# A planner that orders the work behind an attention stage, with new intervals, and a last token tile in two column halves

## The chip, the core and the metric

The kernel runs on one core of one Trainium2 chip. The metric is the device time of one execution, in microseconds. The core's engines, by the names that the profile uses: PE (TensorE, the matmuls; PEld is its weight load), DVE (VectorE), ACT (ScalarE), POOL (GpSimd), and SP, which issues the DMAs here (SPq is its queue). Each engine works through a list of instructions in the order that the program fixed for it, and waits where an instruction's inputs or its buffer are not there yet.

## The reference

A banded attention with a bias over 2 x 8 heads (576 positions, head size 64) gives 1152 tokens of 512 numbers. They pass a mixture of four experts, and then a gated network behind an RMS norm:

```python
def _moe_ref(x, domain_probs, w1, w2):          # x 1152x512, w1 4x512x1024, w2 4x1024x512
    p = domain_probs / (domain_probs.sum(-1, keepdims=True) + 1e-09)
    for e in range(E):
        h = np.maximum(x @ w1[e], 0.0)
        out += p[:, e:e + 1] * (h @ w2[e])

def _moe2_ref(x, w_gate, w_val, w_out, rms_g):  # d_ff 1536
    rms = np.sqrt(np.mean(x * x, axis=-1, keepdims=True) + 1e-06)
    xn = x / rms * rms_g
    g = xn @ w_gate
    silu = g * (1.0 / (1.0 + np.exp(-g)))
    return (silu * (xn @ w_val) @ w_out).astype(np.float32)
```

## The kernel before, in words

**Attention** fills the first 74 us. Its order is written out by hand (class Flow); nothing here touches it.

**Behind it** stand 1152 tokens as 9 tiles of 128. The four experts are done in two halves of the hidden width each, which gives eight units u = 0 to 7. A unit has hidden products (512 hidden columns from all tokens) and out products (`out_plain`: for each token tile 12 matmuls of 128x512 into one bank of PSUM, L1168, which `mix` then adds into y with a weight, L1198). The hidden products of u = 1 to 7 go as Strassen products: `products` (L1032 on) makes four blocks of a 2x2 product from seven block products of six matmuls of 128x288 each (L1050), in four banks `ps_a` to `ps_d`, with sums by DVE between them: `x` and `r` are SBUF tiles that take banks and earlier sums, and the next matmuls of a block wait for its bank to be read (`r<-ps_c,x` is a DVE addition, L798, that reads bank c). Then comes the norm (`finish`, `transposes`, with ACT's Sqrt and Square), and the gated network: its first part, `plain_unit_0`, is plain (`gated`: 12 matmuls of 128x384 from `gemm_in`, L285, for gate and value, Silu on ACT, L1355, a product on DVE, L1359), the rest is Strassen again, and three out products (u = 0 to 2) follow, of which the second and third are added into `acc` by DVE (L798) and the third stored tile by tile (`out_y`, L1420).

**Splits.** Every matmul operand is split in a high part in a short float form, which ACT copies (L802, `wa<-raw`, `wb<-raw`, `xh<-ps_b`), and a low part, which DVE gets by subtraction (L795, `wa<-raw,wa`, `xl<-ps_b,xh`). The weights come by DMA into two buffers `raw`, of 512 KB a load, from `in_w` (the experts') or from `f` (the gated network's). Those of the gated network are 64-bit floats first; ACT and three DVE instructions turn each piece of them (`scratch`) into 32-bit ones in a tile `stage` (L977, then L980, L983 and L986 one on the other's result), and a DMA stores it to `f`.

**What sets the order.** Class `Plan` (L53 to 148) keeps a time for each of PE, DVE, ACT and SP while the program is written. Work that PE's next matmuls wait for is placed at once (`now`, `pe`); splits, weight conversions, norm steps and loads are put down with a due time (`later`) and fill places where the planner expects an engine free (`step`, `drain`). An instruction is taken to occupy its engine for `START` + n x `RATE`, and its result to be there `LAT` after that for whatever needs it:

```python
    LAT = 0.1
    START = {"d": 0.16, "a": 0.19, "q": 0.2}
    RATE = {"d": 1 / 960, "a": 1 / 1200, "q": 0.0025}
```

The planner has no entry for the reload of ACT's function table, which the compiler puts in where the functions of two ACT instructions need different tables (ACT_TABLE_LOAD). What comes out is a fixed list for each engine; no time of the planner is in the kernel itself.

Of the kernel before, what the change touches and what calls it, by code (L numbers as in the profile page):

```python
# [21 lines left out]
NT, DM = B * S, H * D  # L22
# [19 lines left out]
class End:  # L42


    def __init__(self, t=math.inf):
        self.own, self.of = t, None

    @property
    def t(self):
        return self.own if self.of is None else max((x.t for x in self.of), default=0.0)  # L50


class Plan:  # L53

    LAT = 0.1
    START = {"d": 0.16, "a": 0.19, "q": 0.2}
    RATE = {"d": 1 / 960, "a": 1 / 1200, "q": 0.0025}

    def __init__(self, free):
        self.t = 0.0
        self.free = {e: max(0.0, free[e] - free["t"]) for e in "daq"}
        self.jobs = []

    def cost(self, e, n):
        return self.START[e] + n * self.RATE[e]

    def ready(self, needs):
        return max((x.t + self.LAT for x in needs), default=0.0)  # L70

    def best(self, job):
        ready = self.ready(job[2])
        if job[6]:
            ready = max(ready, min(x.t for x in job[6][0]) + self.LAT)
        if ready == math.inf:
            return None
        ends = []
        for e in job[0]:
            start = max(self.free[e], ready)  # L80
            ends.append((start + self.cost(e, job[1]), start, e))
        return min(ends)[1:]

    def step(self, until, only=None, due=None):

# [21 lines left out]
        return True  # L107

    def issue(self, e, n, needs, emit, end):
        start = max(self.free[e], self.ready(needs))  # L110
        emit(e)
        self.free[e] = start + self.cost(e, n)
        end.own = self.free[e] + (2.0 if e == "q" else 0.0)

    def later(self, engines, n, needs, emit, due, buffer=None):

# [2 lines left out]
        return end  # L119

    def settle(self, needs):
        while self.ready(needs) == math.inf:
            assert self.step(math.inf)

    def drain(self, until):
# [1 line left out]
            pass  # L127

    def now(self, e, n, needs, emit, slack=None):
        self.settle(needs)  # L130
        ready = self.ready(needs)
        self.drain(min(ready, max(self.t, self.free[e])))
        while self.step(ready, e):
            pass
        if slack is not None:
            while self.step(max(ready, self.free[e]) + 0.01, e, self.t + slack):
                pass
        end = End()
        self.issue(e, n, needs, emit, end)
        return end  # L140

    def pe(self, n, cols, needs, emit):
        self.settle(needs)
        start = max(self.t, self.ready(needs))
# [80 lines left out]
def tile_fused(ctx: ExitStack, tc: tile.TileContext, qS, kS, vS, probs, w1, w2, wgv, wo, g, out):  # L225
# [585 lines left out]
    class Issued:  # L811


        def __init__(self, end):
            self.end = end

        @property
        def t(self):
            return self.end.t - 2.0 - pl.LAT

    loads = {"raw": [], "t": []}

# [197 lines left out]
    def any_bank(half=0, leave=False):  # L1020

        turn["ps"] += 1
        if leave:
            return bank(min(("bd", "ac")[(turn["pr"] + 1) % 2], key=lambda tag: min(x.t for x in rings[tag])))
        if held or turn["busy"]:
            return bank(("ba", "dc")[half][turn["pr"] % 2])
        tags = ["abcd"[(turn["ps"] + i) % 4] for i in range(4)]
        return bank(min(tags, key=lambda tag: min(x.t for x in rings[tag])))
# [127 lines left out]
            reading[g].append(end)  # L1156
        return w, end, da

    def out_plain(parts, w, t, put, last=()):

        a, end, da = parts
        ps, need, done = any_bank(leave=t > NTT - 3)

        def emit():
            n = 0
            for k in range(4):
                for s, i in ((0, 0), (0, 1), (1, 0)):
                    nc.tensor.matmul(ps, lhsT=a(s)[:, k, :], rhs=w[k][0]()[:, i, :], start=(n == 0), stop=(n == 11))  # L1168
                    n += 1

        k = pl.pe(12, DM, [end, need] + [x[1] for x in w], emit)
        done.of = [put(t, slice(0, DM), ps, [k])]
        da.of = [k]
        for e in last:
            e.of = [k]

    def out_tiles(w, put, parts, ahead, between=lambda t: None, last=()):

        for t in range(NTT):
            for i in range(t, min(t + ahead + 1, NTT)):  # L1180
                if i not in parts:
                    parts[i] = plain_parts(i, pl.t + 2.7 * (i - t))
            out_plain(parts.pop(t), w, t, put, last if t == NTT - 1 else ())
            between(t)
# [110 lines left out]
    for u in range(1, NU):  # L1295
# [173 lines left out]
```

## Time and profile before

| | |
|---|---|
| time, median of 3 runs | 653.48 us (653.34 to 653.51) |
| time of the profiled execution | 653.97 us |
| its span in the profile | 652.2 us |
| PE busy | 644.9 us (99%) |
| DVE busy | 505.8 us (78%) |
| ACT busy | 317.1 us (49%) |
| POOL busy | 43.6 us (7%) |
| granted TensorE clock | 1.00 in every stretch |
| chain that ended last | PE 98%, DMA 1% |

The times in the rows are microseconds from the start of the span. The span is 1.8 us shorter than the profiled execution's own time; the rest lies around the program.

### The profile page before, as it was taken

The numbers are of one execution on the slowest core, as the hardware profiler recorded it, in microseconds if no ns is written. First come the engines' busy times: TensorE is split into PE (matmuls) and PEld (weight loads), VectorE is DVE, ScalarE is ACT, GpSimd is POOL, SyncE is SP. The second block draws the span as 40 slices with busy tenths as digits, with TensorE's granted clock in tenths as the row PEclk, the third lists the DMA queues.
The fourth block names the chain that finished last, engine by engine and source line by source line (L and its number), as shares of the span: only waits on it lengthen the run. The fifth ranks groups of instructions, "written<-read, shape, count | busy, mean of one in ns | idle before, by whom it ended". The sixth has DMA issues, their size and how long they took to land.

```text
span 652.2 us, 11044 instructions
## 1 busy us (share of the span) xinstructions
PE 644.9 (99%) x4166; PEld 583.0 (89%) x4166; DVE 505.8 (78%) x1113; ACT 317.1 (49%) x726; POOL 43.6 (7%) x94
## 2 busy tenths in 40 slices
PE   7999999999999999999999999999999999999997
PEld 5688899989989989889889889889998999899986
DVE  7987677788888898897888887888776388847672
ACT  7988364633635535535435535874445335213330
POOL 6865000000000000000000000000000000000000
PEclk9999999999999999999999999999999999999999
DMA  8542014154433624625525334011111101000012
GB/s 266 172 135 64 1 66 129 33 159 144 165 131 119 207 96 146 193 81 173 167 91 181 101 118 145 32 63 64 66 34 64 65 1 66 33 1 33 33 50 96
DMA packets 24229, 64.95 MB, mean 100 GB/s; under 512 B 2672, under 2 KB 5488, under 8 KB 24176
## 3 DMA queue, kind: packets, MB, share of 16 engines
q1 hardware_dynamic: 23888, 63.96, 29.8%
q8 instruction: 32, 0.52, 0.3%
q10 hardware_dynamic: 288, 0.30, 0.1%
q14 instruction: 21, 0.17, 0.1%
HBM read 52.45 MB, written 11.80 MB: 99 GB/s over the span
## 4 chain that ended last, share of the span: by engine, by line
PE 98%; DMA 1%; DVE 0%; issue 0%; SPq 0%
PE ps_a L1168 14%; PE ps_c L1050 11%; PE ps_d L1050 11%; PE ps_d L1168 9%; PE ps_b L1168 8%; PE ps_c L1168 8%; PE ps_b L1050 8%; PE ps_a L1050 8%; PE ps_b L285 3%; PE a L653 2%; PE ps_c L285 2%; PE pst L550 2%; PE ps_d L285 2%; PE po L569 2%; PE ps_a L285 2%; PE a L684 2%
## 5 line engine op out<-in xcount | busy, mean ns | idle before, releaser
L1168 PE MATMUL ps_a<-wa,op 128*128 128x512 f32 x408 | 96.5, 390 | 0.0
L1168 PEld LDWEIGHTS ps_a<-wa,op 128*128 128x128 f32 x408 | 76.4, 188 | 15.8
L802 ACT ACTIVATE op<-h 128x512 fp32r<-128x512 f32 x95 | 57.6, 626 | 59.0 <-PE ps_d L1168 24.7
L802 ACT ACTIVATE wb<-raw 128x512 fp32r<-128x512 f32 (+1 forms) x98 | 49.9, 536 | 39.8 <-DVE raw L795 39.6
L795 DVE TENSOR_TENSOR op<-h,op 128x512 fp32r<-128x512 f32 x95 | 63.7, 685 | 2.7 <-ACT op L802 2.4
L1168 PE MATMUL ps_d<-wa,op 128*128 128x512 f32 x252 | 59.1, 389 | 0.0
L1168 PE MATMUL ps_b<-wa,op 128*128 128x512 f32 x240 | 56.6, 391 | 0.0
L795 DVE TENSOR_TENSOR wb<-raw,wb 128x512 fp32r<-128x512 f32 (+1 forms) x98 | 54.6, 575 | 2.4 <-ACT wb L802 2.1
L1168 PE MATMUL ps_c<-wa,op 128*128 128x512 f32 x240 | 56.3, 390 | 0.0
L1168 PEld LDWEIGHTS ps_d<-wa,op 128*128 128x128 f32 x252 | 47.2, 188 | 9.8
L1168 PEld LDWEIGHTS ps_c<-wa,op 128*128 128x128 f32 x240 | 45.0, 188 | 9.3
L1168 PEld LDWEIGHTS ps_b<-wa,op 128*128 128x128 f32 x240 | 44.6, 188 | 9.1
L795 DVE TENSOR_TENSOR wa<-raw,wa 128x512 fp32r<-128x512 f32 (+1 forms) x50 | 31.8, 651 | 13.2 <-ACT wa L802 13.2
L1050 PE MATMUL ps_c<-xh,wb 128*128 128x288 f32 x160 | 38.6, 297 | 0.0
L1050 PE MATMUL ps_d<-xh,wb 128*128 128x288 f32 x160 | 38.6, 296 | 0.0
L1050 PE MATMUL ps_a<-xh,wb 128*128 128x288 f32 x160 | 38.3, 294 | 0.0
L1050 PE MATMUL ps_b<-xh,wb 128*128 128x288 f32 x160 | 38.2, 294 | 0.0
L802 ACT ACTIVATE wa<-raw 128x512 fp32r<-128x512 f32 (+1 forms) x50 | 27.8, 597 | 18.6 <-DMA raw<-in_w 16.0
L1111 ACT ACTIVATE h<-r 128x576 f32<-128x576 f32 x28 | 19.2, 686 | 30.8 <-DVE r L798 30.8
L798 DVE TENSOR_TENSOR r<-ps_c,x 128x288 f32<-128x288 f32 x44 | 20.1, 457 | 17.5 <-PE ps_c L1050 15.2
L795 DVE TENSOR_TENSOR raw<-raw 128x256 f32<-128x256 f32 x66 | 27.7, 419 | 0.7
L1050 PEld LDWEIGHTS ps_b<-xh,wb 128*128 128x128 f32 x160 | 27.8, 188 | 0.4
(264 smaller groups left out, 1523.2 us busy)
## 6 DMA issues: line engine op xcount, KB each, us to landing
raw<-in_w SPq DMA_DIRECT2D x32, 512.0 KB, 3.8
scratch<-in_wgv SPq DMA_DIRECT2D x24, 512.0 KB, 4.5
f<-stage SPq DMA_DIRECT2D x36, 256.0 KB, 2.5
raw<-f SPq DMA_DIRECT2D x18, 512.0 KB, 3.2
scratch<-in_wo SPq DMA_DIRECT2D x12, 512.0 KB, 4.5
out_y<-acc SPq DMA_DIRECT2D x9, 256.0 KB, 2.0
vt<-in_vS SPq DMA_DIRECT2D x4, 512.0 KB, 5.4
qt<-in_qS SPq DMA_DIRECT2D x7, 288.0 KB, 4.1
```

The costliest lines, as they stand in the source:

```text
L285: nc.tensor.matmul(ps, lhsT=a, rhs=x[:, k, tok], start=(n == 0), stop=(n == 3 * KC - 1))
L550: nc.tensor.transpose(pst[:w, j, :], tts[n % 2][:, 2 * kb + j, c0 : c0 + w], ident)
L569: nc.tensor.matmul(po[r, kb * P : kb * P + len(range(blocks.shape[1])) * P], lhsT=vt[:, kb, v], rhs=blocks[:, :, 1:3, :] if j else blocks[ ...
L653: nc.tensor.matmul(box[0], lhsT=a, rhs=x[:, k, tok], start=k == 0 and a is wh and x is xh, stop=k == 3 and a is wl)
L684: nc.tensor.matmul(box[0], lhsT=tile[0][:, x, k, :], rhs=v[:, i, :], start=k == 0 and x == i == 0, stop=k == 3 and x == 1)
L795: EN[e].tensor_tensor(out=out, in0=a, in1=b, op=ALU.subtract)
L798: EN[e].tensor_tensor(out=out, in0=a, in1=b, op=ALU.add)
L802: nc.scalar.activation(out=out, in_=a, func=AF.Copy)
L1050: nc.tensor.matmul(ps, lhsT=s[:, k, :], rhs=t(k), start=start and m == 0, stop=m == 5, skip_group_check=True,)
L1111: return wrote(gr, pl.now("a", tok.stop - tok.start, needs + was_reading[gr], lambda e: nc.scalar.activation(out=h[:, c, tok], in_=src, fu ...
L1168: nc.tensor.matmul(ps, lhsT=a(s)[:, k, :], rhs=w[k][0]()[:, i, :], start=(n == 0), stop=(n == 11))
```

## The change

The planner gets other numbers. `LAT` goes from 0.1 to 0.04. `START` becomes `HOLD`, the interval after which the engine takes its next instruction: 0.07 in place of 0.16 for DVE, 0.09 in place of 0.19 for ACT. `MORE` is how much later than that the result is there for another engine: 0.085 for DVE, 0.1 for ACT, 2.0 for a DMA, 0.17 for PE (0 before). A new method `seen` asks which engine needs a result: on the engine that made it, it is taken to be there as soon as that engine takes its next instruction.

```diff
-    LAT = 0.1
-    START = {"d": 0.16, "a": 0.19, "q": 0.2}
+    LAT = 0.04
+    HOLD = {"d": 0.07, "a": 0.09, "q": 0.2}
+    MORE = {"d": 0.085, "a": 0.1, "q": 2.0, "t": 0.17}
     RATE = {"d": 1 / 960, "a": 1 / 1200, "q": 0.0025}
...
+    def seen(self, e):
+
+        if self.of is not None:
+            return max((x.seen(e) for x in self.of), default=0.0)
+        return self.hold if e == self.e and e is not None else self.own + Plan.LAT
...
     def cost(self, e, n):
-        return self.START[e] + n * self.RATE[e]
-
-    def ready(self, needs):
-        return max((x.t + self.LAT for x in needs), default=0.0)
+        return self.HOLD[e] + (n[e] if isinstance(n, dict) else n) * self.RATE[e]
+
+    def ready(self, needs, e):
+        return max((x.seen(e) for x in needs), default=0.0)
...
-        end.own = self.free[e] + (2.0 if e == "q" else 0.0)
+        end.own, end.e, end.hold = self.free[e] + self.MORE[e], e, self.free[e]
...
         self.t = start + n * (cols / 2400 + 0.013)
-        return End(self.t)
+        return End(self.t + self.MORE["t"], "t", self.t)
```

The out products get a width. The last token tile of the last unit (u = 2, tile 8) is done as two halves of 256 columns: 24 matmuls of 128x256 in place of 12 of 128x512, two DVE additions of 128x256, two stores of 128 KB. `out_first` is new too, and nothing calls it.

```diff
-    def out_plain(parts, w, t, put, last=()):
+    def out_plain(parts, w, t, put, last=(), width=DM, leave=False, begun=None):
 
         a, end, da = parts
-        ps, need, done = any_bank(leave=t > NTT - 3)
+        for c0 in range(0, DM, width):
...
+            k = pl.pe(12, width, [end, need] + [x[1] for x in w], emit)
+            done.of = [put(t, c, ps[:, :width], [k])]
...
-        out_tiles(right_o, put, parts, 3, last=o_read)
+        out_tiles(right_o, put, parts, 3, last=o_read, width=DM // 2 if u == NV - 1 else DM)
```

PE's list keeps its order, but for that last tile, and POOL's is the same. The lists of DVE, ACT and SP are ordered anew behind the attention. Line numbers move: L795, L798, L802 of before are L804, L807, L811 of the change; L980, L983, L986 are L992, L995, L998; L1267, L1272, L1355, L1359 are L1303, L1308, L1391, L1395. Three places follow.

**Place A: DVE in the first block product of u = 1**, at about 102 to 109 us. The rows with `ps_b` and `ps_d` are the sums that PE's next block product waits for; the others split weights. Before:

```order
L798 TENSOR_TENSOR x<-ps_b,x 128x288
L798 TENSOR_TENSOR r<-ps_d,x 128x288
L798 TENSOR_TENSOR r<-ps_d,r 128x288
L795 TENSOR_TENSOR wb<-raw,wb 128x512
L795 TENSOR_TENSOR wa<-raw,wa 128x512
L798 TENSOR_TENSOR r<-ps_d,x 128x288
```

With the change:

```order
L804 TENSOR_TENSOR wb<-raw,wb 128x512 x2
L804 TENSOR_TENSOR wa<-raw,wa 128x512 x2
L807 TENSOR_TENSOR x<-ps_b,x 128x288
L804 TENSOR_TENSOR wa<-raw,wa 128x512
L807 TENSOR_TENSOR r<-ps_d,x 128x288
L807 TENSOR_TENSOR r<-ps_d,r 128x288
L804 TENSOR_TENSOR wa<-raw,wa 128x512
```

Two subtractions of `wb` and two of `wa` now stand directly ahead of the sums, and one `wa<-raw,wa` stands between `x<-ps_b,x` and `r<-ps_d,x`.

**Place B: DVE in a hidden product of u = 2**, at about 159 to 171 us; two like it follow in u = 3 and u = 4. L980, L983 and L986 (L992, L995, L998) are the three steps on a `stage`, `op<-h,op` splits the left side of an out product. Before, from `r<-ps_c,r` on (the list then goes on with `x<-ps_d,x`, L983, L980, `x<-ps_a,x`, `r<-ps_c,x`, `r<-ps_c,r`, L986):

```order
L798 TENSOR_TENSOR r<-ps_c,r 128x288
L986 SCALAR_TENSOR_TENSOR stage<-scratch,stage 128x512
L983 SCALAR_TENSOR_TENSOR stage<-scratch,stage 128x512
L798 TENSOR_TENSOR r<-ps_c,x 128x288
L798 TENSOR_TENSOR x<-ps_c,x 128x288
L986 SCALAR_TENSOR_TENSOR stage<-scratch,stage 128x512
L798 TENSOR_TENSOR x<-ps_b,x 128x288
L798 TENSOR_TENSOR r<-ps_d,x 128x288
L798 TENSOR_TENSOR r<-ps_d,r 128x288
L795 TENSOR_TENSOR op<-h,op 128x512 x2
L980 TENSOR_SCALAR stage<-stage 128x512
L798 TENSOR_TENSOR r<-ps_d,x 128x288
```

With the change, the same stretch:

```order
L807 TENSOR_TENSOR r<-ps_c,r 128x288
L995 SCALAR_TENSOR_TENSOR stage<-scratch,stage 128x512
L998 SCALAR_TENSOR_TENSOR stage<-scratch,stage 128x512
L992 TENSOR_SCALAR stage<-stage 128x512
L995 SCALAR_TENSOR_TENSOR stage<-scratch,stage 128x512
L807 TENSOR_TENSOR r<-ps_c,x 128x288
L807 TENSOR_TENSOR x<-ps_c,x 128x288
L998 SCALAR_TENSOR_TENSOR stage<-scratch,stage 128x512
L807 TENSOR_TENSOR x<-ps_b,x 128x288
L807 TENSOR_TENSOR r<-ps_d,x 128x288
L804 TENSOR_TENSOR op<-h,op 128x512
L807 TENSOR_TENSOR r<-ps_d,r 128x288
```

and directly behind it:

```order
L804 TENSOR_TENSOR op<-h,op 128x512
L992 TENSOR_SCALAR stage<-stage 128x512
L995 SCALAR_TENSOR_TENSOR stage<-scratch,stage 128x512
L998 SCALAR_TENSOR_TENSOR stage<-scratch,stage 128x512
L807 TENSOR_TENSOR r<-ps_d,x 128x288
L807 TENSOR_TENSOR x<-ps_d,x 128x288
L992 TENSOR_SCALAR stage<-stage 128x512
L995 SCALAR_TENSOR_TENSOR stage<-scratch,stage 128x512
L807 TENSOR_TENSOR x<-ps_a,x 128x288
L807 TENSOR_TENSOR r<-ps_c,x 128x288
L998 SCALAR_TENSOR_TENSOR stage<-scratch,stage 128x512
L807 TENSOR_TENSOR r<-ps_c,r 128x288
```

Between the first `r<-ps_c,r` and the last `r<-ps_c,x` shown there are now ten steps on a `stage` where there were six, with the same nine sums and the same two splits of `op`; and one step, L998, stands ahead of the last `r<-ps_c,r`, where it (L986) stood behind.

**Place C: ACT and DVE in the plain part of the gated network**, at about 436 to 446 us. `xh` and `xl` are the two parts of the normalized tokens, which PE's next gate and value products read; `y<-y,rstd` scales a token tile; `sg` is Silu, `h` the product behind it. ACT before:

```order
L802 ACTIVATE xh<-ps_c 128x4x128 x2
L1267 ACTIVATE v<-v 128x3
L1355 ACT_TABLE_LOAD
L1355 ACTIVATE sg<-ps_d 128x384
L1272 ACTIVATE y<-y,rstd 128x512 x2
L802 ACTIVATE xh<-ps_b 128x4x128
L802 ACTIVATE xh<-ps_a 128x4x128
L802 ACTIVATE xh<-ps_d 128x4x128
L1355 ACTIVATE sg<-ps_a 128x384
```

ACT with the change:

```order
L1303 ACTIVATE v<-v 128x3
L811 ACTIVATE xh<-ps_c 128x4x128 x2
L1308 ACTIVATE y<-y,rstd 128x512
L1391 ACT_TABLE_LOAD
L1391 ACTIVATE sg<-ps_d 128x384
L1308 ACTIVATE y<-y,rstd 128x512
L811 ACTIVATE wa<-raw 128x512 x2
L811 ACTIVATE xh<-ps_b 128x4x128
L811 ACTIVATE xh<-ps_a 128x4x128
L811 ACTIVATE xh<-ps_d 128x4x128
```

The second scaling and two copies of `wa<-raw` now stand between the Silu `sg<-ps_d` and the three copies of `xh`. DVE before:

```order
L1359 TENSOR_TENSOR h<-ps_b,sg 128x384
L795 TENSOR_TENSOR wb<-raw,wb 128x512 x2
L795 TENSOR_TENSOR xl<-ps_b,xh 128x4x128
L795 TENSOR_TENSOR xl<-ps_a,xh 128x4x128
L795 TENSOR_TENSOR xl<-ps_d,xh 128x4x128
L795 TENSOR_TENSOR scratch<-xh 128x576
```

DVE with the change:

```order
L1395 TENSOR_TENSOR h<-ps_b,sg 128x384
L804 TENSOR_TENSOR wa<-raw,wa 128x512 x2
L804 TENSOR_TENSOR scratch<-xh 128x576
L807 TENSOR_TENSOR scratch<-scratch,xl 128x576
L804 TENSOR_TENSOR xl<-ps_b,xh 128x4x128
L804 TENSOR_TENSOR xl<-ps_a,xh 128x4x128
L804 TENSOR_TENSOR xl<-ps_d,xh 128x4x128
```

Two subtractions of `wa` and two sums into `scratch` stand ahead of the three subtractions of `xl`, where two subtractions of `wb` stood.

## Rows read from the trace of the kernel before

**Rows 1.** Busy time by stretch: us, each engine's busy time (x instructions), PE clock, DMA

```profile
73.90:648.50 574.60, 574.60 (x3425) 528.28 (x3423) 445.86 (x854) 259.55 (x523) 0.00 (x0) 1.00 0.29 95
```

**Rows 2.** The chain that ended last, at the end: start, us, what

```profile
645.81 2.73 PE ps_a L1168 x12
...
648.56 0.69 DVE acc L798
```

**Rows 3.** The page's groups and DMA issues (median us to landing)

```profile
L798 DVE TENSOR_TENSOR r<-ps_c,x 128x288 f32<-128x288 f32 x44 | 20.1, 457 | 17.5 <-PE ps_c L1050 15.2
...
raw<-f SPq DMA_DIRECT2D x18, 512.0 KB, 3.2
...
out_y<-acc SPq DMA_DIRECT2D x9, 256.0 KB, 2.0
```

**Rows 4.** DVE in order of time, 158 to 170 us: start, us, what

```profile
159.56 0.46 DVE L798 TENSOR_TENSOR r<-ps_c,r 128x288 f32<-128x288 f32 x1 [0.32 <-PE ps_c L1050]
159.93 0.68 DVE L986 SCALAR_TENSOR_TENSOR stage<-scratch,stage 128x512 int32<-128x512 int32 x1
...
161.95 0.46 DVE L798 TENSOR_TENSOR r<-ps_c,x 128x288 f32<-128x288 f32 x1 [0.74 <-PE ps_c L1050]
162.44 0.46 DVE L798 TENSOR_TENSOR x<-ps_c,x 128x288 f32<-128x288 f32 x1
...
163.79 0.46 DVE L798 TENSOR_TENSOR x<-ps_b,x 128x288 f32<-128x288 f32 x1 [0.29 <-ACT x L802]
164.36 0.46 DVE L798 TENSOR_TENSOR r<-ps_d,x 128x288 f32<-128x288 f32 x1
...
168.99 0.42 DVE L980 TENSOR_SCALAR stage<-stage 128x512 int32<-128x512 int32 x1
```

**Rows 5.** PE in order of time, two matmuls at 171 to 172 us

```profile
171.30 0.29 PE L1050 MATMUL ps_c<-xh,wb 128*128 128x288 f32 x1
...
172.10 0.96 PE L1050 MATMUL ps_c<-t,wb 128*128 128x288 f32 x6
```

**Rows 6.** ACT in order of time, 436 to 445 us

```profile
436.19 1.09 ACT L802 ACTIVATE xh<-ps_c 128x512 fp32r<-128x512 f32 x2 [1.34 <-PE ps_c L1288]
...
437.39 1.28 ACT L1355 ACT_TABLE_LOAD   x1
438.68 0.50 ACT L1355 ACTIVATE sg<-ps_d 128x384 f32<-128x384 f32 x1
439.07 1.33 ACT L1272 ACTIVATE y<-y,rstd 128x512 f32<-128x512 f32 x2
441.23 0.60 ACT L802 ACTIVATE xh<-ps_b 128x512 fp32r<-128x512 f32 x1 [0.83 <-PE ps_b L1288]
...
444.23 1.15 ACT L802 ACTIVATE wa<-raw 128x512 fp32r<-128x512 f32 x2 [1.04 <-DMA raw<-f]
```

**Rows 7.** DVE in order of time, 439 to 446 us

```profile
439.69 1.28 DVE L795 TENSOR_TENSOR wb<-raw,wb 128x512 fp32r<-128x512 f32 x2
...
443.07 0.68 DVE L795 TENSOR_TENSOR xl<-ps_d,xh 128x512 fp32r<-128x512 f32 x1
...
444.80 0.75 DVE L798 TENSOR_TENSOR scratch<-scratch,xl 128x576 f32<-128x576 f32 x1
445.58 0.76 DVE L795 TENSOR_TENSOR scratch<-scratch,xl 128x576 f32<-128x576 f32 x1
```

**Rows 8.** PE in order of time, one matmul at 444 us

```profile
444.19 0.33 PE L285 MATMUL ps_c<-xl,wb 128*128 128x384 f32 x1
```

**Rows 9.** ACT at 101 us and PE at 108 us, in order of time

```profile
101.33 0.69 ACT L1196 ACTIVATE y<-ps_c,pn_sb 128x512 f32<-128x512 f32 x1 [0.36 <-PE ps_c L1168]
...
107.76 0.29 PE L1050 MATMUL ps_d<-xh,wb 128*128 128x288 f32 x1
```

**Rows 10.** DMA issues in 107 to 109 us, then in 155 to 159 us

```profile
raw<-in_w SPq DMA_DIRECT2D x2, 512.0 KB, 5.5
...
raw<-in_w SPq DMA_DIRECT2D x1, 512.0 KB, 3.6
```

More of the change, by code (lines that the diff above doesn't have):

```diff
@@ L42, with __init__ @@
 class End:
-    def __init__(self, t=math.inf):
+    def __init__(self, t=math.inf, e=None, hold=None):
         self.own, self.of = t, None
+        self.e, self.hold = e, hold
     @property
@@ L63, in __init__ @@
         self.free = {e: max(0.0, free[e] - free["t"]) for e in "daq"}
-        self.jobs = []
+        self.jobs, self.slack = [], None
     def cost(self, e, n):
-        return self.START[e] + n * self.RATE[e]
-    def ready(self, needs):
-        return max((x.t + self.LAT for x in needs), default=0.0)
+        return self.HOLD[e] + (n[e] if isinstance(n, dict) else n) * self.RATE[e]
+    def ready(self, needs, e):
+        return max((x.seen(e) for x in needs), default=0.0)
     def best(self, job):
[L73 to L77, printed above, removed]
         ends = []
         for e in job[0]:
+            ready = self.ready(job[2], e)
+            if job[6]:
+                ready = max(ready, min(x.seen(e) for x in job[6][0]))
             start = max(self.free[e], ready)
             ends.append((start + self.cost(e, job[1]), start, e))
-        return min(ends)[1:]
+        end = min(ends)
+        return None if end[0] == math.inf else end[1:]
     def step(self, until, only=None, due=None):
@@ L109, in issue @@
     def issue(self, e, n, needs, emit, end):
-        start = max(self.free[e], self.ready(needs))
+        start = max(self.free[e], self.ready(needs, e))
         emit(e)
         self.free[e] = start + self.cost(e, n)
-        end.own = self.free[e] + (2.0 if e == "q" else 0.0)
+        end.own, end.e, end.hold = self.free[e] + self.MORE[e], e, self.free[e]
     def later(self, engines, n, needs, emit, due, buffer=None):
@@ L121, in settle @@
     def settle(self, needs):
-        while self.ready(needs) == math.inf:
+        while self.ready(needs, None) == math.inf:
             assert self.step(math.inf)
@@ L129, in now @@
     def now(self, e, n, needs, emit, slack=None):
+        slack = self.slack if slack is None else slack
+        slack = self.slack if slack is None else slack
         self.settle(needs)
-        ready = self.ready(needs)
+        ready = self.ready(needs, e)
         self.drain(min(ready, max(self.t, self.free[e])))
@@ L143, in pe @@
         self.settle(needs)
-        start = max(self.t, self.ready(needs))
+        start = max(self.t, self.ready(needs, "t"))
         self.drain(start)
@@ L818, in t, with seen @@
         def t(self):
-            return self.end.t - 2.0 - pl.LAT
+            return self.end.t - Plan.MORE["q"] - pl.LAT
+        def seen(self, e):
+            return self.end.t - Plan.MORE["q"]
     loads = {"raw": [], "t": []}
@@ L1157, in plain_parts, with emit, out_tiles, out_first @@
         return w, end, da
-    def out_plain(parts, w, t, put, last=()):
+    def out_plain(parts, w, t, put, last=(), width=DM, leave=False, begun=None):
         a, end, da = parts
-        ps, need, done = any_bank(leave=t > NTT - 3)
+        for c0 in range(0, DM, width):
+            ps, done = begun or (None, None)
+            need = End(0.0)
+            if not begun:
+                ps, need, done = any_bank(leave=leave)
+            c = slice(c0, c0 + width)
+            def emit():
+                n = 0
+                for k in range(4):
+                    for s, i in ((0, 0), (0, 1), (1, 0)):
+                        nc.tensor.matmul(ps[:, :width], lhsT=a(s)[:, k, :], rhs=w[k][0]()[:, i, c], start=not (n or begun), stop=(n == 11))
+                        n += 1
+            k = pl.pe(12, width, [end, need] + [x[1] for x in w], emit)
+            done.of = [put(t, c, ps[:, :width], [k])]
+        da.of = [k]
+        for e in last:
+            e.of = [k]
+    def out_tiles(w, put, parts, ahead, between=lambda t: None, last=(), width=DM, tiles=(0, NTT), begun={}):
+        for t in range(*tiles):
+            for i in range(t, min(t + ahead + 1, tiles[1])):
+                if i not in parts:
+                    parts[i] = plain_parts(i, pl.t + 2.7 * (i - t))
+            end = t == NTT - 1
+            out_plain(parts.pop(t), w, t, put, last if end else (), width if end else DM, t > tiles[1] - 3, begun.get(t))
+            between(t)
+    def out_first(parts, w, tag, last):
+        a, end, da = parts
+        ps, need, done = bank(tag)
         def emit():
@@ L1167, in emit @@
                 for s, i in ((0, 0), (0, 1), (1, 0)):
-                    nc.tensor.matmul(ps, lhsT=a(s)[:, k, :], rhs=w[k][0]()[:, i, :], start=(n == 0), stop=(n == 11))
+                    nc.tensor.matmul(ps, lhsT=a(s)[:, k, :], rhs=w[k][0]()[:, i, :], start=(n == 0), stop=False)
                     n += 1
         k = pl.pe(12, DM, [end, need] + [x[1] for x in w], emit)
-        done.of = [put(t, slice(0, DM), ps, [k])]
         da.of = [k]
@@ L1175, in out_plain @@
             e.of = [k]
[L1177 to L1184, printed above, removed]
+        return ps, done
     mixed = {}
@@ L1231, in tile_fused @@
             parts[t + 2] = plain_parts(t + 2, pl.t + 2)
-        out_plain(parts.pop(t), v, t, lambda *a: mix(0, *a), [w2_read] if t == NTT - 1 else [])
+        out_plain(parts.pop(t), v, t, lambda *a: mix(0, *a), [w2_read] if t == NTT - 1 else [], leave=t > NTT - 3)
     ss = const.tile([P, NTT], F32, name="ss")
```

## The prediction

> **What bounds the kernel now.** I read the busy time by stretch first. Behind the attention, from 73.9 to 648.5 us, PE is busy for 574.60 of 574.60 us at a granted clock of 1.00 [rows 1]. So in this stretch there is no idle time of PE that a better order of the other engines could take away, and none that could swallow a new wait: as PE's list keeps its order and its shapes up to the last token tile, each 0.1 us by which a sum, a split or a load comes late at PE is 0.1 us at the end. DVE with 528.28 us comes close, but it is not the bound. Next I read the end of the chain of waits: the last 12 matmuls take 2.73 us from 645.81, the last addition on DVE 0.69 us from 648.56, and the store (median 2.0 us from issue to landing) fills nearly all that is left up to 652.2 [rows 2, 3]. Only here can time be won. For the new order I then took the three places where the lists of the change put other work ahead of something that PE needs soon, and walked along them with the durations of before.
>
> **The tail, part by part.** Twelve matmuls of 512 columns take 2.73 us, 0.2275 each [rows 2]; six of 288 take 172.10 - 171.30 = 0.80, 0.133 each [rows 5]. On the line through both, one of 256 takes 0.133 - 32 x 0.00042 = 0.120, and 24 take 2.88: PE ends 0.15 later. The addition that remains behind it has 256 columns in place of 512. Between 457 ns at 288 and 690 at 512 [rows 2, 3] the slope is 1.04 ns a column, so it takes 0.42: 0.27 earlier. The first half's addition and store have 1.4 us of matmuls to lie behind. The last store moves 128 KB in place of 256. At worst its 2.0 us stay, at best it shrinks as from 512 KB (3.2) to 256 KB (2.0) [rows 3], by half of 1.2, 0.6. The number of its rows stays 128 and only their length is halved, so I stand nearer to the first: 0.2. The sum is 0.15 - 0.27 - 0.2 = **-0.3 us** (-0.1 to -0.7).
> The Trainium skill, "Perfetto Trace Analysis", section DMA Optimizations, speaks against this: small DMAs (under 2 KB) have significant overhead for each transfer. The halved rows are 1 KB long. By it the store would keep its 2.0 us and the tail would win 0.1; no row of before shows a store of such rows.
>
> **Place C, 436 to 446 us, once.** Before, ACT made `xh<-ps_c` twice and the root from 436.19 to 437.39, then the table reload (1.28), then Silu at 438.68; `xh<-ps_b` waited 0.83 us for PE and started at 441.23 [rows 6]; the subtractions followed, the last one `xl<-ps_d` from 443.07 for 0.68, to 443.75 [rows 7]; PE took its result at 444.19 [rows 8]. That is 0.44 of slack. With the change ACT's list reads: root and two `xh` (to 437.39), `y<-y,rstd` (0.61: two take 1.33 and the second of a pair runs out in some 0.7), reload 438.00 to 439.28, Silu (0.39 to the next, from 438.68 to 439.07), second `y` at 439.67, `wa<-raw` at 440.28 and, 0.52 on (a pair takes 1.15, one 0.63), at 440.80, and the three `xh` only then, from 441.32, 0.50 apart [rows 6]. The load for these `wa` isn't late: its buffer comes free 6 us sooner, as two subtractions of `wb` that followed Silu (439.69) [rows 7] now stand ahead of the norm. DVE's list has two `wa` first: the first copy ends at 440.91, so 440.93 and 0.60 on 441.53 (a pair takes 1.28, one 0.68), then a sum into `scratch` at 442.13, and one that needs its result 0.78 on, at 442.91 (444.80 to 445.58 in the rows), then 0.68 with the change of operands `xl<-ps_b` 443.59, `xl<-ps_a` 444.19, `xl<-ps_d` 444.79, done 445.47 [rows 7]. PE starts some 0.05 later, at 445.52 against 444.19: **1.3 us**. If the two sums went at 0.60 and 0.60 it would be 1.0; if the second scaling takes 0.70 and the sums 0.78, 1.5. What makes it late is that the reload, 1.28 us, isn't in the planner's numbers, and that the margins which covered it (0.16 and 0.19 an instruction) are halved.
> The Trainium skill, "ScalarE: Activation LUTs", section What ACT_TABLE_LOAD costs, gives 1283 ns for a reload and another 1380 ns for a drain with each switch. The reload agrees with the row to the digit (1.28), the drain doesn't: Silu follows the reload within 0.01 us here [rows 6]. By the rule with its drain place C would cost 2.7 (estimate from that page).
>
> **Place B, 159 to 171 us, in u = 2, 3 and 4.** I start at `r<-ps_c,r`, 159.56, which waits for PE in both lists. Intervals: a sum 0.37 to the next instruction (159.56 to 159.93), 0.49 to a sum that needs it (161.95 to 162.44), 0.57 from an `x` to the `r` that needs it (163.79 to 164.36), a step of 512 or a split 0.60, with its dependent step behind it 0.72 (0.68 and a wait), L980 0.45 to the step that needs it (0.42 and a wait) [rows 4, 7]. The list of the change gives: 159.93 L995, 160.65 L998, 161.25 L992, 161.70 L995, 162.30 `r<-ps_c,x` (161.95 before), 162.79 `x<-ps_c,x`, then as before 1.35 to `x<-ps_b,x`, 164.14, `r<-ps_d,x` 164.71, split 165.08, `r<-ps_d,r` 165.68, split 166.05, L992 166.65, L995 167.10, L998 167.82, `r<-ps_d,x` 168.42, `x` 168.91, L992 169.28, L995 169.73, `x<-ps_a,x` 170.33, `r<-ps_c,x` 170.90, done 171.36. PE then starts at 171.41; before it did so at 171.30 [rows 5]. L998 follows at 171.27, and with it ahead of it `r<-ps_c,r` goes from 171.87 to 172.33; PE at 172.38, where 172.10 + 0.11 was due [rows 5]: 0.17 more. That is 0.28 a unit, 0.84 for three; in u = 5 to 7 one split stands where L992 and L995 precede `x<-ps_a,x`, and no step between the two `r<-ps_c`, so the walk is 0.45 shorter there and I take nothing but 0.03 each: **0.9 us**. Of four added steps (some 2.4 us) 1.5 goes into waits of DVE for PE (0.32 and 0.74 among them [rows 4]). If dependent steps go at 0.60 nothing is left; if each step takes 0.02 more, 0.4 a unit: 0 to 1.2.
>
> **Place A, 102 to 109 us, once.** A `wa<-raw,wa` stands ahead of `r<-ps_d,x`, and its `raw` must land first. The load is issued when the two `wb` subtractions have freed the buffer. Their copies stand ahead of ACT's `y<-ps_c`, 101.33 [rows 9], so they end at about 102.3. A load of 512 KB alone takes 3.6 us, one of a pair 5.5 [rows 10] (3.2 is the median from `f` [rows 3]); SP's list has a load shortly ahead of this one and another shortly behind, so I take 4.4, between the two: landed 106.7. Behind it come the copy 0.65, the subtraction 0.62, the sum 0.46 and PE's 0.05: 108.5 against 107.76 [rows 9], **0.8 us** (0 at 3.6, 1.9 at 5.5). All else that waits on DVE there waits too, the next sums among it, but PE needs them later.
>
> **The sum.** 0.8 + 0.9 + 1.3 - 0.3 = +2.7 us. Against the profiled execution's own 653.97 us that is 656.7, of a span of 654.9; that execution lies 0.5 above the median of the three runs, 653.48, so I predict **656.2 us**. The bounds add up to +0.3 (A and B nothing, C 1.0, tail -0.7) and +4.5.
>
> **The rivals.**
> *The planner's intervals hold (not slower).* If a dependent instruction on the same engine starts after the shorter interval and a load lands in 3.5 us, A and B leave nothing. C keeps about 1.2 of its reload: +0.9, 654.4 us, within what a measurement of this kernel can tell from no change (0.2%, 1.3 us). It decides from a sum of stalls below 1.6. For it: at B only 0.1 to 0.2 is missing, and at A all hangs on one load. Against it: 0.78 from one `scratch` sum to the next, which the shorter interval would make 0.67 [rows 7]. If ACT found a gap for the reload as well, 653.2.
> *Loads land late.* At 5.5 A costs 1.9, so 657.3; with another late load elsewhere 658 and more. For it: the pair of rows 10 and ACT's wait of 1.04 for `raw<-f` [rows 6]. Against it: the queue of before is mostly free.
> *The reload costs twice.* ACT could be emptied around a reload at a place where, other than before, a scaling stands directly ahead of it: once more its 1.28 us [rows 6], place C 2.6, 657.5. Silu's start at 438.68, right behind the reload, speaks against it. This is what the Trainium skill's page "ScalarE: Activation LUTs" says of the drain, above.
> *Faster.* The tail alone, with the best store, gives 652.8, which isn't 1.3; for more PE would have to run closer than in rows 1, at full busy time.
>
> **How the numbers follow.** The forecast with stalls at two or three places has 0.62, the planner's intervals 0.17, late loads 0.14, the reload twice 0.04, a gain beyond the tail 0.03. The first has 655.0 to 657.0 as its own range. To leave out no more than 2 in 10 the range goes from 654.6 (near the rival without A and B) to 657.9 (A at its upper end, 657.3, and 0.6 for a second late load): the unknown costs make it 3.3 wide. Slower by over 0.2% are the forecast, late loads and the reload, 0.80; within it the planner's intervals, 0.17; faster 0.03.
>
> **What would show it.** In the trace of the changed kernel PE should have idle time before `ps_c<-xl` at C of 1.0 to 1.5, released by DVE's `xl<-ps_d`; before a matmul into `ps_d` at A of 0 to 1.9, released by `r<-ps_d,x` with ACT's `wa<-raw` waiting for `raw<-in_w` ahead of it; and three pairs of 0.1 and 0.2 in u = 2 to 4 before `ps_c`, released by `r<-ps_c`. From the end of PE to the end of the span it should be 0.3 to 0.6 shorter. The prediction is wrong if PE is still busy throughout, if PE waits at places that I haven't walked, or if the waits of ACT in those stretches are longer than the loads of the rows.

## The result, and the profile after

The changed kernel takes 658.61 us (median of 6 runs, 657.91 to 659.29) against 653.50 us before (6 runs, 653.30 to 653.61): the ratio is 1.0076 (95% interval 1.0065 to 1.0087). It is slower, as forecast, but by 5.1 us where 2.7 were forecast, and above the range. The profiled execution of the change is the fastest of the six, 657.91 us.

The page's head, of the change:

```profile
span 656.1 us, 11108 instructions
...
PE 647.6 (99%) x4178; PEld 584.5 (89%) x4178; DVE 501.5 (76%) x1116; ACT 315.7 (48%) x724; POOL 43.5 (7%) x94
```

DVE has less to do, not more (501.5 us against 505.8), and the attention ends no later: the stretch behind it begins at 73.4 us, where it began at 73.9 [rows 1]. Busy time by stretch, of the change (columns as in [rows 1]):

```profile
73.40:106.90 33.50, 33.50 (x202) 30.50 (x200) 23.90 (x42) 19.42 (x39) 0.00 (x0) 1.00 0.28 90
106.90:110.00 3.10, 1.79 (x14) 1.56 (x13) 2.11 (x4) 1.45 (x3) 0.00 (x0) 1.00 0.13 54
110.00:172.00 62.00, 62.00 (x393) 57.75 (x392) 50.94 (x100) 29.93 (x61) 0.00 (x0) 1.00 0.45 139
172.00:174.50 2.50, 2.44 (x18) 2.07 (x17) 2.02 (x4) 1.24 (x3) 0.00 (x0) 1.00 0.65 226
174.50:441.00 266.50, 266.50 (x1536) 239.67 (x1536) 222.19 (x432) 129.91 (x264) 0.00 (x0) 1.00 0.40 123
441.00:450.00 9.00, 7.89 (x50) 7.54 (x50) 7.36 (x13) 5.53 (x10) 0.00 (x0) 1.00 0.19 58
450.00:653.10 203.10, 203.10 (x1238) 190.34 (x1236) 133.07 (x264) 70.71 (x142) 0.00 (x0) 1.00 0.12 42
```

PE is idle at places A (1.31 us), B (0.06) and C (1.11), at an unchanged clock. The view of PE's waits has two entries in this time:

```profile
PE ps_d L1062 <- DVE r L807: 1.3, 1, 1.3
PE ps_c L294 <- DVE xl L804: 1.1, 1, 1.1
```

That is 2.4 us, less than half of what is lost, and here the reading by idle time ends. A matmul of 288 columns is recorded as 0.29 us long, but in a full stream the next starts after 0.133 [rows 5]; a wait of up to 0.16 us leaves no gap in the records, only a longer interval between two starts. So I went through the starts of all matmuls behind the attention and took from each interval that of the full stream; what is left over is called a late start below. (The transposes of the norm, 128 columns wide, start at the same distances in both kernels and are left out.) Place A, in order of time (ACT, DVE, PEld, then PE):

```profile
106.96 1.15 ACT L811 ACTIVATE wa<-raw 128x512 fp32r<-128x512 f32 x2 [2.27 <-DMA raw<-in_w]
...
107.62 0.69 DVE L804 TENSOR_TENSOR wa<-raw,wa 128x512 fp32r<-128x512 f32 x1 [1.99 <-ACT wa L811]
108.23 0.45 DVE L807 TENSOR_TENSOR r<-ps_d,x 128x288 f32<-128x288 f32 x1
...
108.73 0.19 PEld L1062 LDWEIGHTS ps_d<-xh,wb 128*128 128x128 f32 x1 [1.54 <-DVE r L807]
...
107.14 0.29 PE L1062 MATMUL ps_b<-xh,wb 128*128 128x288 f32 x1
108.74 0.40 PE L1062 MATMUL ps_d<-xh,wb 128*128 128x288 f32 x1 [1.31 <-DVE r L807]
108.97 0.29 PE L1062 MATMUL ps_d<-xl,wb 128*128 128x288 f32 x1
```

From 107.14 to 108.74 are 1.60 us: a wait of 1.47. From there to the second matmul are 0.23 in place of 0.133: **another 0.10**, called the restart below. The row of PEld says why: the weights of the first matmul are loaded at 108.73, when the wait is over, while in a full stream they are loaded during the matmul before. The first matmul's recorded start hides that load, its length (0.40 for 0.29) and the second matmul show it. Place B, u = 2 (DVE, then PE):

```profile
170.92 0.69 DVE L995 SCALAR_TENSOR_TENSOR stage<-scratch,stage 128x512 int32<-128x512 int32 x1
171.53 0.45 DVE L807 TENSOR_TENSOR x<-ps_a,x 128x288 f32<-128x288 f32 x1
172.08 0.46 DVE L807 TENSOR_TENSOR r<-ps_c,x 128x288 f32<-128x288 f32 x1
172.46 0.68 DVE L998 SCALAR_TENSOR_TENSOR stage<-scratch,stage 128x512 int32<-128x512 int32 x1
173.05 0.45 DVE L807 TENSOR_TENSOR r<-ps_c,r 128x288 f32<-128x288 f32 x1
...
172.24 0.29 PE L1062 MATMUL ps_a<-xh,wb 128*128 128x288 f32 x1
172.59 0.40 PE L1062 MATMUL ps_c<-xh,wb 128*128 128x288 f32 x1
172.83 0.29 PE L1062 MATMUL ps_c<-xl,wb 128*128 128x288 f32 x1
...
173.37 0.29 PE L1062 MATMUL ps_c<-xh,wb 128*128 128x288 f32 x1
173.56 0.67 PE L1062 MATMUL ps_c<-t,wb 128*128 128x288 f32 x3
```

Two waits, 0.22 and 0.06, each with its restart of 0.10. Place C (ACT, DVE, PEld, PE), which answers to [rows 6 to 8]:

```profile
440.56 1.28 ACT L1391 ACT_TABLE_LOAD   x1
441.86 0.49 ACT L1391 ACTIVATE sg<-ps_d 128x384 f32<-128x384 f32 x1
442.25 0.71 ACT L1308 ACTIVATE y<-y,rstd 128x512 f32<-128x512 f32 x1
442.86 1.14 ACT L811 ACTIVATE wa<-raw 128x512 fp32r<-128x512 f32 x2
443.90 0.59 ACT L811 ACTIVATE xh<-ps_b 128x512 fp32r<-128x512 f32 x1
...
447.38 0.68 DVE L804 TENSOR_TENSOR xl<-ps_d,xh 128x512 fp32r<-128x512 f32 x1
...
448.12 0.19 PEld L294 LDWEIGHTS ps_c<-xl,wb 128*128 128x128 f32 x1 [1.43 <-DVE xl L804]
...
446.50 0.51 PE L294 MATMUL ps_c<-xh,wb 128*128 128x384 f32 x2
448.12 0.44 PE L294 MATMUL ps_c<-xl,wb 128*128 128x384 f32 x1 [1.11 <-DVE xl L804]
448.40 0.51 PE L294 MATMUL ps_c<-xh,wb 128*128 128x384 f32 x2
```

Two matmuls from 446.50 (0.17 apart) should be followed at 446.84; 448.12 is 1.27 later. At none of the three places were the weights what PE waited for. At A and B it is the sum that still reads the bank, at C the tokens `xl`, while the loaded operand is `wb`; the weight load stands behind the same wait all the same. Whether it could be done during the wait was not tried. Over all starts, wait and restart together:

| place | waits of PE | us |
|---|---|---|
| A | 1 | 1.57 |
| B, u = 2, 3, 4 | 6 | 0.49 + 0.41 + 0.41 = 1.31 |
| the same place in u = 5, 6, 7 | 3 | 3 x 0.16 = 0.49 |
| C | 1 | 1.38 |
| 546 us (two) and 604 us, in the later Strassen products | 3 | 0.31 + 0.08 = 0.39 |
| sum | 14 | 5.14 |

Thirteen of the 14 are a late first matmul with a restart of 0.10 behind it. At 604 us the first matmul starts on time, and only the second is late, by 0.08.

The end of the chain, of the change, and the last store (median us to landing):

```profile
650.26 2.88 PE ps_a L1185 x24
653.15 0.02 issue
653.17 0.42 DVE acc L807
```

```profile
out_y<-acc SPq DMA_DIRECT2D x1, 128.0 KB, 1.7
```

PE's last tile takes 0.15 more than the 2.73 of before, the last addition 0.27 less than 0.69 [rows 2], and from its end to the end of the span (656.13 and 652.17 to two places) pass 656.13 - 653.59 = 2.54 us in place of 652.17 - 649.25 = 2.92. Tail: -0.50. With the 5.14 that is +4.6; the stretch began 0.5 earlier in this execution, so +4.1, and the spans differ by 4.0.

### The profile page after: what moved, and what is told of

It is laid out like the page before. It is cut to its first block, busy times and chain, and to the rows that moved or that the text cites. A ratio compares the mean times of both kernels' runs of the same rounds, so it can differ in the third digit from the quotient of the medians.

```text
span 656.1 us, 11108 instructions
## 1 busy us (share of the span) xinstructions
PE 647.6 (99%) x4178; PEld 584.5 (89%) x4178; DVE 501.5 (76%) x1116; ACT 315.7 (48%) x724; POOL 43.5 (7%) x94
## 4 chain that ended last, share of the span: by engine, by line
PE 90%; DVE 5%; ACT 2%; DMA 1%; issue 1%; SPq 0%; DVEq 0%; ACTq 0%
PE ps_a L1185 12%; PE ps_c L1062 10%; PE ps_d L1062 10%; PE ps_d L1185 8%; PE ps_b L1185 8%; PE ps_c L1185 8%; PE ps_b L1062 7%; PE ps_a L1062 7%; PE a L662 2%; PE pst L559 2%; PE po L578 2%; PE ps_b L294 2%; PE ps_c L294 2%; PE a L693 2%; PE s L492 2%; PE ps_d L294 2%
## 5 line engine op out<-in xcount | busy, mean ns | idle before, releaser
L1185 PE MATMUL ps_a<-wa,op 128*128 128x512 f32 (+1 forms) x420 | 96.7, 384 | 0.0
L811 ACT ACTIVATE op<-h 128x512 fp32r<-128x512 f32 x95 | 57.9, 625 | 36.4 <-PE ps_d L1185 16.8
L804 DVE TENSOR_TENSOR op<-h,op 128x512 fp32r<-128x512 f32 x95 | 64.6, 683 | 1.6 <-ACT op L811 1.3
L811 ACT ACTIVATE wb<-raw 128x512 fp32r<-128x512 f32 (+1 forms) x98 | 50.3, 537 | 27.3 <-DVE raw L804 27.0
L804 DVE TENSOR_TENSOR wb<-raw,wb 128x512 fp32r<-128x512 f32 (+1 forms) x98 | 54.7, 574 | 1.1 <-ACT wb L811 1.1
L804 DVE TENSOR_TENSOR wa<-raw,wa 128x512 fp32r<-128x512 f32 (+1 forms) x50 | 31.3, 653 | 20.3 <-ACT wa L811 20.3
L811 ACT ACTIVATE wa<-raw 128x512 fp32r<-128x512 f32 (+1 forms) x50 | 27.8, 597 | 31.1 <-DMA raw<-in_w 26.8
L807 DVE TENSOR_TENSOR r<-ps_c,x 128x288 f32<-128x288 f32 x44 | 20.0, 456 | 18.4 <-PE ps_c L1062 16.6
L1062 PEld LDWEIGHTS ps_d<-xh,wb 128*128 128x128 f32 x160 | 27.9, 188 | 1.5 <-DVE r L807 1.5
L811 ACT ACTIVATE x<-ps_b 128x288 f32<-128x288 f32 x22 | 8.8, 402 | 42.0 <-PE ps_b L1062 42.0
```

The lines of the kernel that those rows point to most:

```text
L804: EN[e].tensor_tensor(out=out, in0=a, in1=b, op=ALU.subtract)
L807: EN[e].tensor_tensor(out=out, in0=a, in1=b, op=ALU.add)
L811: nc.scalar.activation(out=out, in_=a, func=AF.Copy)
L1062: nc.tensor.matmul(ps, lhsT=s[:, k, :], rhs=t(k), start=start and m == 0, stop=m == 5, skip_group_check=True,)
L1185: nc.tensor.matmul(ps[:, :width], lhsT=a(s)[:, k, :], rhs=w[k][0]()[:, i, c], start=not (n or begun), stop=(n == 11))
```

## The experiments

Two theories. *Waits theory:* all the loss is in these 14 waits and the restarts behind them; they come from the new order at each place, and taking one away gives its time back. *Rivals:* the time comes back as a wait elsewhere; or the halves, or the shorter intervals as such, cost it.

**e1_halves**: the planner of before, with the column halves alone (the diff of `out_plain` above, without the rest).

```diff
-        out_tiles(right_o, put, parts, 3, last=o_read)
+        out_tiles(right_o, put, parts, 3, last=o_read, width=DM // 2 if u == NV - 1 else DM)
```

> The planner of before, and only the last token tile in two column halves. Waits theory (all that the change loses it loses in waits of PE that the new order makes; the tail wins what the traces show from the start of the last matmul group to the end of the span, 6.56 us before and 6.00 after): 652.9 us, 0.56 below before, PE without a wait. By the prediction's own term for the tail: 653.2, 0.3 below. If the halves cost something that the waits hide: 653.5 or more.

653.25 us, ratio 0.9998 (0.9990 to 1.0007): no loss. The span of its profile ends 6.03 us behind the start of the last matmul group (6.52 before, 6.03 with the change; the expectation had worked with spans to one place), so the tail is 0.5 shorter in the traces. The spans of its eleven runs say the same, 651.2 us in the median against 651.7 before. The times give only 0.2 and can't tell that from nothing: what lies outside the span took 1.8 to 2.5 us in this kernel, where it took 1.7 to 1.9 before; why, stays open.

**e2_order**: the change without the halves (that line undone).

> The planner of the change, without the two column halves. Waits theory: the same waits of PE as with the change, and the tail of before: 659.1 us, 0.5 above the change. If the halves are part of what is lost: 658.6 or less.

658.31 us, ratio 1.0074 (1.0062 to 1.0087). The late starts in its trace sum to 5.15, at the same places. The whole loss is the new order's. That it came out 0.3 below the change and not 0.5 above it lies within the spread of both (658.0 to 658.9, 657.9 to 659.3).

**e_a_wait**: the change, place A alone.

```diff
...
-                ends.append(parts_of(512, ..., [hr, need], due))
+                ends.append(parts_of(512, ..., [hr, need, End(wait if out else 0.0)], due))
...
-    nxt = load_w2(W2[1], pl.t + 29)
+    nxt = load_w2(W2[1], pl.t + 29, pl.t + 20)
```

> The change, with one edit at place A: the two splits of the second load of u = 1 are not placed before a time that lies behind the block product. Nothing else moves but what follows from that. Waits theory: PE's wait of 1.47 us before the block product in ps_d goes, with the 0.10 by which the matmul behind it comes late; 657.0 us if the profiled execution of the change is typical. As that one is the fastest of six (657.91 against a median of 658.61), and what differs between them is taken to be how late this load lands, some 656.5, with the runs within 0.4 us of one another in place of 1.4. Rival (the splits are then late elsewhere, and PE waits there): 658.6 as with the change.

656.42 us (656.33 to 656.70), ratio 1.0045 (1.0032 to 1.0059): 2.2 below the change in the median, with five runs within 0.4 us. PE is busy all through the stretch in which it idled 1.31 us:

```profile
105.00:110.00 5.00, 5.00 (x40) 5.00 (x39) 2.27 (x5) 0.85 (x2) 0.00 (x0) 1.00 0.08 31
```

All other waits of the table stayed. So A costs 1.57 us in the change's profile and, by the medians, some 2.2 in a usual run; the largest in a trace is 1.94 (e_b_late). What moves it is the load: in the four traces that have place A, it took 4.7, 5.0, 5.0 and 5.4 us to land (e3_reload, e2_order, the change, e_b_late), and PE waited 1.18, 1.43, 1.47 and 1.83 us. So most of the change's spread of 1.4 us is taken to be A's.

This run also clears one of the load's two neighbours in the queue. The load behind is issued 1.2 us after the one at A in the change, but 10.7 us after it here, and the one at A landed no sooner. In e_hold (below) the load at A is issued when the one ahead, `scratch<-in_wgv`, has only 0.9 us to go instead of 2.8. The load at A (us from issue to landing) in the change, here and in e_hold:

```profile
raw<-in_w SPq DMA_DIRECT2D x1, 512.0 KB, 5.0
...
raw<-in_w SPq DMA_DIRECT2D x1, 512.0 KB, 5.1
...
raw<-in_w SPq DMA_DIRECT2D x1, 512.0 KB, 4.1
```

**e3_reload**: the change, with the reload counted at the one Silu that has it (1536 columns at ACT's rate of 1/1200 us are 1.28 us).

```diff
...
-        j = pl.now("a", T, [k, n, roots[0]], lambda e: nc.scalar.activation(out=f, in_=pg[:, :T], func=AF.Silu))
+        j = pl.now("a", T + reload, [k, n, roots[0]], lambda e: nc.scalar.activation(out=f, in_=pg[:, :T], func=AF.Silu))
...
-            k = gated(w, c, tok, lambda: transposes(*((4, 5), (6, 7, 8), ())[i]) if c == 0 else None)
+            k = gated(w, c, tok, lambda: transposes(*((4, 5), (6, 7, 8), ())[i]) if c == 0 else None, 1536 if n == 0 else 0)
```

> The change, where the planner counts 1.28 us more for the one Silu ahead of which the function table is reloaded. Waits theory: place C loses its wait of 1.27 us and the 0.10 behind it, all else stays: 657.2 us. Rival (the reload only moves the wait to another operand of the gate and value products, since the same work must be done in the same time): 658.0 or more.

656.39 us (655.98 to 658.67), ratio 1.0051 (1.0038 to 1.0064). C's wait is gone from the trace, and with it the two at 546 us (1.38 + 0.31); A was 1.28 in this profile, 0.29 less than in the change's. Together that is 1.98 us, and the two profiled executions lie 1.93 apart. The median fell by 2.2, which takes in A's spread.

```profile
441.00:450.00 9.00, 9.00 (x58) 8.95 (x57) 8.25 (x15) 5.66 (x11) 0.00 (x0) 1.00 0.16 58
```

**e_b_late**: the change, place B alone.

```diff
...
-                ends.append(store(src, dst, start, start + 20))
+                ends.append(store(src, dst, start + (extra if m == 5 else 0.0), start + 20))
...
-            store_next(6 if u < 4 else 5, pl.t + 24)
+            store_next(6 if u < 4 else 5, pl.t + 24, 20.0)
```

> The change, with one edit at place B: in u = 2 to 4 the last of six weight conversions may not start before the block product is over, so that DVE's list there reads as in u = 5 to 7. Waits theory: of the two waits a unit the second goes and the first shrinks to that of u = 5 to 7 (0.05 and the 0.10 behind it); 0.83 us in all by the trace of the change, 657.8 us in the median, with place A as loose as with the change. In the trace: three waits of 0.16 where there were six, place A and C as before. Rival (the waits at B are PE's own, the conversions don't matter): 658.6 and the same six waits.

657.32 us (657.18 to 660.11), ratio 1.0065 (1.0053 to 1.0077). The second wait of each unit is gone; the first is 0.13 in u = 2 and 0.05 in u = 3 and 4, each with its 0.10: 0.76 us less by the trace. The median fell by 1.3, with A as loose as before (1.94 in this profile), so only the trace tells this one.

**e5_load**: the change, with a load taken to land later.

```diff
-    MORE = {"d": 0.085, "a": 0.1, "q": 2.0, "t": 0.17}
+    MORE = {"d": 0.085, "a": 0.1, "q": 3.5, "t": 0.17}
```

> The change, where the planner takes a load to land 3.5 us after its issue in place of 2.0. Waits theory: place A goes (some 2.2 us in the median run, 1.57 in the profile), and with the conversions placed later place B and its likes too (1.8); what stays is place C, 1.38, and one or two waits of 0.1 to 0.2 behind 540 us: 654.5 us, runs within 0.5 us. Rival (each new list has as many waits as this one, since the intervals are too short everywhere): 657 or more.

654.60 us (654.38 to 654.77), ratio 1.0017 (1.0008 to 1.0025). A and B are gone but for one late start of 0.04; C stands with 1.27 + 0.11, and one of 0.07 at 601 us. The sum, 1.5, less the tail's 0.5 is the 1.1 us measured, to 0.1.

**e_r_three**: the kernel before, with one sum done three times, so that PE waits in many places of another kind.

```diff
-            j = pl.now("d", n, [kd], lambda e: add(e, y1, pd, x))
+            j = pl.now("d", n, [kd], lambda e: [add(e, y1, pd, x) for _ in range(3)])
```

> The kernel before, where one sum of each Strassen product (the first sum from bank d that its second half makes) is done three times instead of once, with the same result; PE then waits for the sums behind it in some 38 places, for 0.1 to 0.6 us each. Restart theory (each wait of PE costs its length and then 0.10 us more, since the weights of the first matmul behind it are loaded only when the wait is over): 7 us of waits and 3.9 of restarts, 664.4 us; in the trace the second matmul behind each wait starts 0.10 late. Rival (the 0.10 is a peculiarity of the places in the change): 660.6, and no late second matmul.

664.91 us, ratio 1.0173 (1.0160 to 1.0186). PE, in order of time:

```profile
118.68 0.29 PE L1050 MATMUL ps_b<-xh,wb 128*128 128x288 f32 x1
118.97 0.40 PE L1050 MATMUL ps_d<-xh,wb 128*128 128x288 f32 x1
119.21 0.29 PE L1050 MATMUL ps_d<-xl,wb 128*128 128x288 f32 x1
...
123.06 0.96 PE L1050 MATMUL ps_c<-t,wb 128*128 128x288 f32 x6
124.04 0.40 PE L1050 MATMUL ps_a<-xh,wb 128*128 128x288 f32 x1
124.28 0.29 PE L1050 MATMUL ps_a<-xl,wb 128*128 128x288 f32 x1
```

0.24 from the first matmul behind a wait to the second, again with the first recorded as 0.40 long. It is so 41 times, 0.105 late on average, 4.3 us together; all late starts make 11.75 us, and 11.4 were measured. Without the restarts the late starts would have been 7.4. The restart belongs to the wait, not to the places of the change.

**e_hold**: the change, with intervals 0.03 us longer.

```diff
-    HOLD = {"d": 0.07, "a": 0.09, "q": 0.2}
+    HOLD = {"d": 0.1, "a": 0.12, "q": 0.2}
```

> The change, with the intervals (HOLD) 0.03 us longer: 0.10 for DVE and 0.12 for ACT in place of 0.07 and 0.09. Margin theory (the change's intervals leave no margin over those of the chip, and dependent steps on one engine, loads and the reload take the rest): with 0.03 for each instruction nearly all waits go, 653.0 us, and none longer than 0.2 in the trace. Rival (the reload and the load times are what is missing, and a few hundredths don't bring 1.3 us): place A or C stays, 654.4 or more.

653.26 us, ratio 0.9998 (0.9989 to 1.0006). Late starts of 0.10 and 0.05 are left (171 and 543 us); A and C are gone too.

**e_abc**: e_a_wait, e_b_late and e3_reload together.

> The change with the three local edits together: the second load's splits at A after the block product, the last conversion at B after it, the reload counted at C. Waits theory (the places add up, each on its own): what stays are six waits of 0.05 and the 0.10 behind each (0.9 us) and one of 0.1 behind 600 us, against a tail that is 0.5 shorter in the traces and 0.2 in the times: 653.9 us (653.7 to 654.3), runs within 0.9 us like those of before. Rival (what is taken away at one place comes back at another): 655 or more.

653.99 us (653.80 to 654.33), ratio 1.0008 (0.9999 to 1.0017). Six waits at `ps_c` and one of 0.09 at 600 us are left, 1.1 us in all, and nothing came back elsewhere. By the traces the places add up: 5.14 less 1.57 for A, 0.76 for B and 1.69 for the reload leaves 1.12. (The medians of the three single runs fell by more in all, 2.2 + 1.3 + 2.2 where this one fell by 4.6.)

**e4_own**: the change without its rule for the own engine.

```diff
-        return self.hold if e == self.e and e is not None else self.own + Plan.LAT
+        return self.own if e == self.e and e is not None else self.own + Plan.LAT
```

> The change without one of its rules: a result is taken to be there for its own engine, too, only when the instruction is over, not when the engine takes its next one. All other numbers as in the change. If that rule is what makes A and B late: the waits there go, and since the reload at C is still not counted some 1.6 us stay there, perhaps at another operand than now: 654.7 us. Rival (the shorter intervals do it, the rule is nothing): A and B as with the change, 658 or more.

654.29 us, ratio 1.0013 (1.0005 to 1.0022). A, B and the waits behind 540 us are gone. C has one, now before another operand:

```profile
443.46 0.34 PE L294 MATMUL ps_d<-xh,wb 128*128 128x384 f32 x1
444.81 0.44 PE L294 MATMUL ps_d<-xl,wb 128*128 128x384 f32 x1 [1.01 <-DVE xl L804]
```

**e6_three**: the change, with the reload, the own engine and the loads as in e3_reload, e4_own and e5_load.

> The change with its intervals as they are (0.07 and 0.09), but with the three things counted that they leave out: the reload (1.28), a result's own engine (ready when the instruction is over), the landing of a load (3.5 in place of 2.0). Waits theory: no wait of PE over 0.15, 653.2 us, level with the halves alone. Rival (only longer intervals for all instructions help): 654.5 or more.

653.11 us, ratio 0.9997 (0.9988 to 1.0006), no late start of PE. The change's intervals can stay as short as they are once the three omissions are counted. This is the best that the runs gave, and it can't be told from before; with PE's stream full, only the tail is left to win.

## Why the prediction was wrong, point by point

- **What bounds the kernel: right.** PE's stream was full before, each wait lengthens the end, the clock stayed at 1.00, and the order gave nothing back.
- **A wait's price: this step failed.** I let PE start 0.05 us behind its release and lost nothing after it, so that a wait cost its length alone. Thirteen of the 14 waits cost a restart of 0.10 on top, 1.4 us together. The Trainium skill, "TensorE: Matmul & The Clock Gate", section LDWEIGHTS (loading the stationary operand), gives a weight load P / 1.2 ns, by P columns: 107 ns for 128. That agrees with the restarts here, 0.102 to 0.107 us and 0.104 on average. A record of PEld is longer, 0.19 us. That a wait exposes the whole load is what the rows show.
- **Place A: the mechanism right, the term mis-sized; this is the other step that failed.** From the landing to PE I had 1.8 us, and it is 1.78 (106.96 to 108.74). But the load took 5.0 us from its issue at 101.89, where I took 4.4 from between 3.6 and 5.5. By the medians A takes 2.2 with its restart, where I had 0.8. The neighbour behind the load isn't what makes it late (e_a_wait). The one ahead may be: the load took 4.1 and 4.0 us in e_hold and e5_load, where that one had nearly landed. No run moves it alone, so this stays open.
- **Place B: right in kind.** 0.28 in u = 2 (0.28 forecast), 0.20 in u = 3 and 4, 0.05 to 0.06 in u = 5 to 7 (0.03 forecast), without restarts. The second wait of a unit hangs on one step on a `stage`, as e_b_late shows.
- **Place C: right.** 1.27 for 1.3, released by `xl<-ps_d`, and counting the reload takes it away.
- **Places that I hadn't walked:** 0.39 us at 546 and 604 us, restarts included.
- **The tail:** PE +0.15 and the addition -0.27 as worked out; the store -0.38 where I took -0.2. The Trainium skill's rule on small DMAs ("Perfetto Trace Analysis", DMA Optimizations) gives those under 2 KB a significant overhead for each transfer. The prediction read it as a store that would keep its 2.0 us, and that reading is not borne out: the 128 KB in rows of 1 KB landed in 1.7 us, the 256 KB in rows of 2 KB in 2.0. As half the bytes took well over half the time, the rule itself is not refuted. Three kernels with the halves and full streams (e1_halves, e_hold, e6_three) lie 0.2 to 0.35 us below before in time, each with an interval that takes in no change.
- **The sum:** on top of 2.7, A +1.4 (2.2 for 0.8), the other 12 restarts +1.25, the unwalked places without theirs +0.2, B -0.1, the tail -0.2: 5.25, where 5.1 were measured. That the sum closes so well rests on the 2.2, which is a difference of medians and stands in no trace.
- **Rivals:** late loads (657.3, with 658 and more for another) was the nearest, and it is part of what happened. The reload did not cost twice: 440.56 + 1.28, and Silu at 441.86. That the planner's intervals hold fails at A and B, yet narrowly: 0.03 an instruction (e_hold), the own-engine rule (e4_own) or later loads (e5_load) each clear both to within 0.10 us. No single number of the change is the cause of A and B; what is gone is the margin that had covered dependent steps and loads. For C it is the reload, which the shorter margins no longer cover.

## What to carry to other kernels

Where the busiest engine's stream is full, as PE's is here, an order computed from exact intervals has nothing to win and stands one uncounted thing (a table reload, a step that waits for its own engine, a load with neighbours) from losing: count these before the margin is cut, or leave the margin. Price a wait of PE as its length and a weight load more, and look for waits in the distance between matmul starts: idle time showed 2.4 of 5.1 us here. An order that hangs on a load can show in the spread of the runs as well (1.4 us here, and 0.4 in e_a_wait, with the load out of the way).

## What the runs showed of the hardware

- Behind a wait of PE, of 0.05 us or of 1.5, the second matmul starts 0.10 late, 13 times in the change and 41 times in e_r_three: the first matmul's weights are loaded only once the wait is over, though at A, B and C it is not the weights that were waited for.
- A load of 512 KB took 3.6 us to land alone [rows 10], 4.0 and 4.1 when the one ahead of it had 0.8 and 0.9 us to go at its issue (e5_load, e_hold), and 4.7 to 5.4 when that one had 2.3 to 2.8 to go (the change, e2_order, e3_reload, e_b_late, e_a_wait).
- With such a load on PE's path the six runs of the change spread over 1.4 us, without it the five of e_a_wait over 0.4. It is not the only thing that spreads: one run each of e4_own and e6_three, which have no wait at A, lies 0.9 and 1.5 above the next.
- From the scaling ahead of the reload (439.82 to 440.54) through it to Silu (441.86) ACT stood idle for 0.02 us on either side.
